# First layer's weight decode: words in PSUM, ranked first and in program order, eight staging areas

## The chip, the cores and the metric

One core of a Trainium2 chip runs the whole program in one launch. The metric is the device time in microseconds (us), the median over runs. Engines are named as in the profile: PE (matmul), PEld (its weight loads), DVE (VectorE), ACT (ScalarE), POOL (GpSimd), SP (SyncE, which here issues every DMA).

## The reference

Three stages follow one another, in fp32:

```python
for t in range(768):                       # 4 batches x 8 heads, head size 40
    y[:, :, t] = r_t @ state
    Sa = state @ a_t
    state = state * w_t - outer(Sa, b_t) + outer(v_t, k_t)
x = y.transpose(0, 2, 1, 3).reshape(3072, 320)
h = x @ w_in                               # first layer, 320 -> 2048, weights float64
x = (h * cos(h)) @ w_out                   # 2048 -> 320, float64
P = exp(x @ w_gate - max); 8 rounds of row and column normalisation
out = sum_e P[:, e] * (relu(x @ w1[e]) @ w2[e])    # second layer, 8 experts, 320 -> 1024 -> 320
```

## The kernel before

The recurrence is cut into 24 chunks of 32 steps. A chunk has three parts: `early(n)` (L664) loads its inputs, scans the decays, forms small matrices, writes them to DRAM and reads them back (tensor `LD`), and has POOL invert them with 62 instructions (`inverse`, L707; result through DRAM tensor `UD`); `late(n)` (L722) fetches that result and builds transposed operands; `chain(n)` (L764) runs the matmuls that carry the state from chunk to chunk, and ends with two stores to the DRAM tensor `XT` (recorded as group "y").

The first layer works in 12 passes of 256 tokens, `moe1(i)` (L940). Pass i needs the `XT` of chunks 2i and 2i+1, and all 16 weight slots `wt1`. Per pass PE does 128 matmuls 128x256 (`l1`) and 96 of 128x320 (`l2`); results go to the DRAM tensor `ZD`. Its work buffers lie in the tiles `fs` and `r2`.

The weights of the first layer arrive as float64 words. `moe1_weights` (L852) decodes 32 blocks, 16 of `w_in` (128x384) and 16 of `w_out` (128x320), in turn. A block is loaded by one DMA into a staging area; `decode` (L535) takes five DVE instructions and one ACT instruction, with an intermediate `t` that lies beside the words in the staging area; ACT rounds the upper part, PE subtracts it from the exact sum by three matmuls into a PSUM bank of pool "A" (`low`, L866), and ACT copies the rest. There are three staging areas, two in `fs` and one in `at2`; the last eight blocks use only the one in `at2` (`PREP_FS`, L575), because `fs` is the passes' by then.

The second layer (`moe2`, L1069) runs 8 experts x 6 groups of 512 tokens on the same engines, after the passes.

Nothing is issued in the order of the code. `Recorder` collects all operations with their dependences, and `order` (L353) plans each engine's order by list scheduling with costs of its own: at each step the engine that is free first takes, of its ready operations, the one with the smallest key. The key is made of the group's entry in `PRIORITY` (L578): first the rank, then, where the second entry is a number, the negative length of the longest path behind the operation (plus that many thousand ns), and where it is None, the operation's place in the program:

```python
r, base, slope = PRIORITY.get(o[6]) or PRIORITY[o[6][0]]
key.append((r, i, 0) if base is None else (r, -tail[i] - 1e3 * (base + slope * o[6][1]), i))
```

PSUM banks are given out in the same plan: pool "A" has four, for the attention, the decode and the second layer's first products; "M" and "N" have two each. Where the plan has PE idle before 800 us, it puts filler matmuls there (`fill`, 64x64 from the constants). The chip then runs each engine's list in that order, each instruction waiting for its semaphores; SP's list is in order too, so a DMA that waits holds back all DMAs behind it. All instructions are issued from one line (L519), so the profile tells them apart by tiles: `XT<-at` is a chunk's result, `ZD<-fs` a pass's, `fs<-in_win`, `at<-in_win`, `fs<-in_moe_w_out` and `at<-in_moe_w_out` are loads of float64 blocks.

Of the kernel before, what the change touches and what calls it, by code (L numbers as in the profile page):

```python
# [6 lines left out]
F32 = mybir.dt.float32  # L7
F32R = mybir.dt.float32r
# [113 lines left out]
class Lazy:  # L122


    def __init__(self, get, sample, region, chain=()):
        self.get, self.sample, self.reg, self.chain = get, sample, region, chain
# [408 lines left out]
def decode(nc, expo, st, t, rest=None, sign=1):  # L535

    lo, hi = st[:, :, 0], st[:, :, 1]
    e = t.bitcast(I32)
    nc.vector.tensor_scalar(e, hi, 20, 0x7FF, op0=ALU.logical_shift_right, op1=ALU.bitwise_and)
    nc.scalar.activation(e, e, AF.Relu, scale=float(2 ** 23), bias=expo)  # L540
    nc.vector.scalar_tensor_tensor(e, hi, -2 ** 31, e, op0=ALU.bitwise_and, op1=ALU.bitwise_or)
    nc.vector.tensor_scalar(hi, hi, 3, 0x7FFFFF, op0=ALU.logical_shift_left, op1=ALU.bitwise_and)
    nc.vector.tensor_tensor(hi, hi, e, op=ALU.bitwise_or)
    rest = t if rest is None else rest
    nc.vector.scalar_tensor_tensor(rest, lo.bitcast(mybir.dt.uint32), sign * 2.0 ** -52, t, op0=ALU.mult, op1=ALU.mult)
    return hi.bitcast(F32), rest


def sinkhorn(nc, ident, P, sk, red, ones, bank):
# [22 lines left out]
        nc.vector.tensor_tensor(P, P, red.unsqueeze(1).to_broadcast([128, 24, 8]), op=ALU.mult)  # L572


PREP_FS = 24  # L575


PRIORITY = {  # L578
    "chain": (0, 0, 0), "y": (1, 0, 0), "early": (1, 0, 0), "late": (1, 0, 0), "prep": (1, 275, 0),
    "one": (1, 0, 0), "gate": (2, 0, 0), "two": (3, None, 0), "fetch": (4, None, 0),  # L580
}
SLOT = 1280
NR1 = 10
# [5 lines left out]
R2_COLS = 1536 + 2048 + 40  # L589
# [3 lines left out]
class Kernel:  # L593
    def __init__(self, sb, ps, dr, a):
        self.a, self.dr = a, dr
        tile = lambda n, c, dt: sb.tile([128, c], dt, tag=n, name=n)
        r1a = tile("r1a", NR1 * SLOT, F32R)
        r1b = tile("r1b", ACC_COLS, F32R)
        self.r2 = tile("r2", R2_COLS, F32R).bitcast(F32)
        self.fs = tile("fs", FS_COLS, F32)  # L600
        self.cst = tile("cst", CONSTS.shape[1], F32)
        self.at1 = tile("at1", AT1_COLS, F32)
        self.at2 = tile("at2", AT2_COLS, F32)
        self.flag = tile("flag", NCH + 2, F32)
        self.nc = nc = Recorder(ps, {"A": (4, 5, 6, 7), "M": (0, 1), "N": (2, 3)}, {x.name for x in a.values()})
        slots = lambda t, n: [t[:, SLOT * i:SLOT * i + SLOT] for i in range(n)]
        ra, rb = slots(r1a.bitcast(F32), NR1), slots(r1b.bitcast(F32), 6)
        self.wt1 = ra + rb
        self.acc = nc.later(r1b, F32, lambda: tile("r1b", ACC_COLS, F32)).rearrange("p (t d) -> p t d", d=DM)
        z = nc.later(self.at1, F32R, lambda: tile("at1", AT1_COLS, F32R)).bitcast(F32)  # L610
        self.zT_all = z[:, 0:ZT_COLS].rearrange("p (t k c) -> p t k c", t=6, k=6)
        self.w2s = [z[:, ZT_COLS + SLOT * i:ZT_COLS + SLOT * i + SLOT] for i in range(NAT)] + ra
        nc.sync.dma_start(out=self.cst, in_=a["consts"])
        self.c = {k: self.cst[:, o:o + w] for k, (o, w) in CONST_COLS.items()}
        nc.fill(self.c["ident"])
        ui = self.c["uinit"]
        self.uinit = bass.AP(ui.tensor, ui.offset + 28, [ui.ap[0], [-4, 8], [1, C]])
        self.nident = tile("nident", 128, F32R)
        self.XT = dr.tile([DM, NT], F32, name="XT")
        self.ZD = dr.tile([NT, DM], F32, name="ZD")  # L620
# [231 lines left out]
    def moe1_weights(self):  # L852

        nc, a = self.nc, self.a
        sets = [self.fs[:, 0:1152], self.fs[:, 1152:2304], self.st]
        self.used = 0

        def stage():
            k = self.used % 3 if self.used < PREP_FS else 2
            self.used += 1  # L860
            return sets[k]

        nident = self.nident
        nc.scalar.activation(nident, self.c["ident"], AF.Copy, scale=-1.0)

        def low(A, hi, Bl):  # L866

            ps = nc.bank("A")[:, 0:A.shape[1]]
            nc.tensor.matmul(ps, lhsT=self.c["ident"], rhs=A, start=True, stop=False)
            nc.tensor.matmul(ps, lhsT=nident, rhs=hi, start=False, stop=False)  # L870
            nc.tensor.matmul(ps, lhsT=nident, rhs=Bl, start=False, stop=True)
            return ps

        for f in range(16):
            nc.group = ("prep", f)
            w = self.wt1[f]
            s = stage()
            st = s[:, 0:768].bitcast(I32).rearrange("p (c w) -> p c w", w=2)
            nc.sync.dma_start(
                out=s[:, 0:768].bitcast(I32), in_=a["win"].bitcast(I32)[f])  # L880
            A, Bl = decode(nc, self.c["expo"], st, s[:, 768:1152], w[:, 384:768].bitcast(F32R), -1)
            hi = w[:, 0:384].bitcast(F32R)
            nc.scalar.activation(hi, A, AF.Copy)
            ps = low(A, hi, Bl)
            nc.scalar.activation(w[:, 384:640].bitcast(F32R), ps[:, 0:256], AF.Copy)
            nc.scalar.activation(w[64:128, 256:384].bitcast(F32R), ps[64:128, 256:384], AF.Copy)
            s = stage()
            st = s[:, 0:640].bitcast(I32).rearrange("p (c w) -> p c w", w=2)
            nc.sync.dma_start(out=s[:, 0:640].bitcast(I32), in_=a["moe_w_out"].bitcast(I32)[128 * f:128 * f + 128, :])
            A, Bl = decode(nc, self.c["expo"], st, s[:, 640:960], w[:, 960:1280].bitcast(F32R), -1)  # L890
            hi, lo = w[:, 640:960].bitcast(F32R), w[:, 960:1280].bitcast(F32R)
            nc.scalar.activation(hi, A, AF.Copy)
            nc.scalar.activation(lo, low(A, hi, Bl), AF.Copy)
# [417 lines left out]
```

## Time and profile before

| | |
|---|---|
| median of 3 runs | 2336.92 us (2335.42 to 2342.84) |
| profiled execution | 2336.27 us |
| its span, first to last instruction | 2334.5 us |
| busy: PE, DVE, ACT, POOL | 98%, 45%, 35%, 29% |

Times in the trace are us from the span's start. A view by windows gives, for each stretch, the busy us and the number of instructions of every engine, then PE's granted clock (1.00 is full), the DMA engines' busy share and GB/s. A view by groups gives the engine, the operation, the tiles written and read, the shape and count, and then busy us, mean ns of one, and the idle time in front. SPq rows are DMA issues: start, us that the issue took, tiles. PE's busy time holds the filler, so it is not all work.

### The profile page before, as it was taken

The numbers are of one execution on the slowest core, as the hardware profiler recorded it, in microseconds if no ns is written. First come the engines' busy times: TensorE is split into PE (matmuls) and PEld (weight loads), VectorE is DVE, ScalarE is ACT, GpSimd is POOL, SyncE is SP. The second block draws the span as 40 slices with busy tenths as digits, with TensorE's granted clock in tenths as the row PEclk, the third lists the DMA queues.
The fourth block names the chain that finished last, engine by engine and source line by source line (L and its number), as shares of the span: only waits on it lengthen the run. The fifth ranks groups of instructions, "written<-read, shape, count | busy, mean of one in ns | idle before, by whom it ended". The sixth has DMA issues, their size and how long they took to land.

```text
span 2334.5 us, 45995 instructions
## 1 busy us (share of the span) xinstructions
PE 2278.6 (98%) x18893; PEld 2082.4 (89%) x18893; DVE 1057.3 (45%) x2106; ACT 820.9 (35%) x1710; POOL 685.8 (29%) x1694
## 2 busy tenths in 40 slices
PE   8999999999999999999999999999999999999997
PEld 8899898898998998899998888999999999999886
DVE  7667888778887654511222222222222222222222
ACT  4436565466655655324112112112112112112111
POOL 5867766588746613002002002002002002001000
PEclk9999998999998999999999999999999999999998
DMA  6434343434443215001001001001001001000000
GB/s 172 111 100 113 88 116 81 98 91 105 100 97 80 64 48 143 6 1 51 1 1 50 1 1 51 1 1 51 1 1 50 1 1 50 1 1 7 23 23 24
DMA packets 155497, 116.86 MB, mean 50 GB/s; under 512 B 112528, under 2 KB 134032, under 8 KB 153360
## 3 DMA queue, kind: packets, MB, share of 16 engines
q1 hardware_dynamic: 155280, 113.86, 19.4%
q8 instruction: 150, 2.46, 0.5%
q14 instruction: 67, 0.55, 0.1%
HBM read 95.73 MB, written 18.09 MB: 49 GB/s over the span
## 4 chain that ended last, share of the span: by engine, by line


## 5 line engine op out<-in xcount | busy, mean ns | idle before, releaser
L519 DVE SCALAR_TENSOR_TENSOR r<-ps,r 128x512 fp32r<-128x512 f32 x384 | 265.3, 691 | 972.2 <-ACT r L519 971.7
L519 PE MATMUL ps<-r1a,r 128*128 128x320 f32 x4248 | 672.4, 310 | 1.7 <-ACT fs L519 1.6
L519 PEld LDWEIGHTS ps<-r1a,r 128*128 128x128 f32 x4248 | 637.5, 188 | 17.4 <-ACT fs L519 2.3
L519 ACT ACTIVATE r<-ps 128x512 fp32r<-128x512 f32 x480 | 286.1, 596 | 1032.1 <-PE ps L519 1009.5
L519 POOL TENSOR_TENSOR at<-at 128x60 f32<-128x60 f32 (+24 forms) x1488 | 545.4, 367 | 261.3 <-DMA at<-LD 123.2
L519 PE MATMUL ps<-at,r1a 128*128 128x512 f32 x2352 | 578.7, 397 | 0.0
L519 PEld LDWEIGHTS ps<-at,r1a 128*128 128x128 f32 x2352 | 436.2, 188 | 94.1 <-issue 0.2
L519 PE MATMUL ps<-at 128*64 128x72 f32 (+6 forms) x6064 | 458.1, 252 | 17.5 <-DVE at L519 6.5
L519 PEld LDWEIGHTS ps<-at 80*64 80x64 f32 (+4 forms) x6064 | 394.1, 150 | 63.3 <-DVE at L519 9.6
L519 POOL TENSOR_TENSOR r1a<-at,r1a 128x256 fp32r<-128x256 f32 (+2 forms) x147 | 101.2, 691 | 832.9 <-ACT r1a L519 823.6
L519 PE MATMUL ps<-at,r 128*128 128x320 f32 (+1 forms) x1128 | 182.4, 313 | 0.0
L519 PEld LDWEIGHTS ps<-at,r 128*128 128x128 f32 (+1 forms) x1128 | 167.3, 184 | 9.7
L519 PE MATMUL ps<-cst 128*64 128x64 f32 x2520 | 167.2, 225 | 4.6 <-DMA cst<-in_consts 4.6
L519 PEld LDWEIGHTS ps<-cst 128*64 128x64 f32 x2520 | 156.5, 140 | 14.0 <-issue 7.4
L519 PE MATMUL ps<-r,r1a 128*128 128x256 f32 x960 | 139.2, 294 | 2.2 <-DVE r L519 2.2
L519 ACT ACTIVATE at<-ps 80x320 f32<-80x320 f32 (+4 forms) x234 | 92.4, 416 | 126.2 <-PE ps L519 123.5
L519 POOL TENSOR_TENSOR at<-at,at 128x256 fp32r<-128x256 f32 (+2 forms) x45 | 31.0, 692 | 348.3 <-ACT at L519 346.6
L519 PEld LDWEIGHTS ps<-r,r1a 128*128 128x128 f32 x960 | 126.2, 197 | 4.7 <-DVE r L519 3.3
L519 DVE TENSOR_TENSOR at<-ps,at 80x160 f32<-80x160 f32 (+4 forms) x396 | 100.7, 316 | 21.0 <-ACT at L519 20.6
L519 ACT ACTIVATE at<-at,cst 64x256 f32<-64x256 f32 (+3 forms) x160 | 88.7, 584 | 39.2 <-PE ps L519 20.5
L519 DVE SCALAR_TENSOR_TENSOR r1b<-ps,fs,r1b 128x320 f32<-128x320 f32 x168 | 80.9, 544 | 36.9 <-PE ps L519 36.9
L519 DVE SCALAR_TENSOR_TENSOR fs<-ps,fs 128x512 f32<-128x512 f32 x96 | 65.8, 685 | 53.1 <-ACT fs L519 52.5
(74 smaller groups left out, 1458.8 us busy)
## 6 DMA issues: line engine op xcount, KB each, us to landing
at<-in_w SPq DMA_DIRECT2D x64, 352.0 KB
at<-in_tabk SPq DMA_DIRECT2D x24, 640.0 KB
at<-LD SPq DMA_DIRECT2D x96, 128.0 KB
at<-in_trv SPq DMA_DIRECT2D x24, 480.0 KB
at<-in_tw SPq DMA_DIRECT2D x24, 165.3 KB
at<-in_nv SPq DMA_DIRECT2D x48, 80.0 KB
ZD<-fs SPq DMA_DIRECT2D x24, 160.0 KB
at<-ZD SPq DMA_DIRECT2D x24, 160.0 KB
```

What stands on the lines that cost most here:

```text
L519: getattr(getattr(nc, self.ENGINES[e]), method)(*[res(x) for x in args], **{n: res(x) for n, x in kwargs.items()})
```

## The change

The decode's intermediate `t` moves from the staging area to a bank of PSUM pool "A". Staging areas shrink to 768 columns and become eight: three in `fs`, four in the tile of `r2`, one in `at2`, used in turn for all 32 blocks; `r2` becomes the passes' buffer once its last staging use is over. In the plan the decode ("prep") gets rank 0 and program order instead of rank 1 with 275 us of advance; the passes ("one") go from rank 1 to rank 0, and keep the order by path length.

```diff
-PREP_FS = 24
 PRIORITY = {
-    "chain": (0, 0, 0), "y": (1, 0, 0), "early": (1, 0, 0), "late": (1, 0, 0), "prep": (1, 275, 0),
-    "one": (1, 0, 0), "gate": (2, 0, 0), "two": (3, None, 0), "fetch": (4, None, 0),
+    "chain": (0, 0, 0), "y": (1, 0, 0), "early": (1, 0, 0), "late": (1, 0, 0), "prep": (0, None, 0),
+    "one": (0, 0, 0), "gate": (2, 0, 0), "two": (3, None, 0), "fetch": (4, None, 0),
 }
@@ Kernel.__init__
-        self.r2 = tile("r2", R2_COLS, F32R).bitcast(F32)
+        self.raw = tile("r2", R2_COLS, F32)
...
+        self.r2 = nc.later(self.raw, F32R, lambda: tile("r2", R2_COLS, F32R)).bitcast(F32)
@@ moe1_weights
-        sets = [self.fs[:, 0:1152], self.fs[:, 1152:2304], self.st]
+        sets = [t[:, 768 * i:768 * i + 768] for t, n in ((self.fs, 3), (self.raw, 4), (self.st, 1)) for i in range(n)]
...
         def stage():
-            k = self.used % 3 if self.used < PREP_FS else 2
             self.used += 1
-            return sets[k]
+            return sets[self.used % len(sets)]
...
-            A, Bl = decode(nc, self.c["expo"], st, s[:, 768:1152], w[:, 384:768].bitcast(F32R), -1)
+            A, Bl = decode(nc, self.c["expo"], st, nc.bank("A", False)[:, 0:384], w[:, 384:768].bitcast(F32R), -1)
...
-            A, Bl = decode(nc, self.c["expo"], st, s[:, 640:960], w[:, 960:1280].bitcast(F32R), -1)
+            A, Bl = decode(nc, self.c["expo"], st, nc.bank("A", False)[:, 0:320], w[:, 960:1280].bitcast(F32R), -1)
```

## Rows read from the trace of the kernel before

**Rows 1.** Windows: length, then busy us (instructions) by engine, PEclk, DMA share, GB/s.
```profile
core 0: us, PE busy (x) PEld busy (x) DVE busy (x) ACT busy (x) POOL busy (x), PEclk, DMA share, GB/s
0.00:60.00 60.00, 53.84 (x881) 50.32 (x882) 45.04 (x86) 26.92 (x64) 32.18 (x74) 0.97 0.67 168
60.00:140.00 80.00, 79.92 (x1150) 71.46 (x1151) 54.49 (x135) 36.58 (x90) 63.21 (x162) 1.00 0.43 110
140.00:300.00 160.00, 152.35 (x2180) 140.65 (x2178) 121.38 (x265) 87.56 (x204) 112.14 (x273) 0.99 0.43 104
300.00:835.00 535.00, 512.29 (x6381) 488.68 (x6377) 421.47 (x912) 312.67 (x703) 345.78 (x992) 0.96 0.38 89
835.00:906.00 71.00, 70.21 (x517) 67.18 (x516) 38.21 (x63) 46.90 (x90) 23.08 (x35) 1.00 0.33 98
```
**Rows 2.** PE groups of 0 to 300 us: the filler, and the passes' first products.
```profile
L519 PE MATMUL ps<-cst 128*64 128x64 f32 x2108 | 138.3, 225 | 4.6 <-DMA cst<-in_consts 4.6
L519 PE MATMUL ps<-r,r1a 128*128 128x256 f32 x128 | 19.7, 296 | 1.5 <-DVE r L519 1.5
L519 PE MATMUL ps<-r,r1b 128*128 128x256 f32 x48 | 7.6, 292 | 0.0
```
**Rows 3.** The same groups of 300 to 835 us.
```profile
L519 PE MATMUL ps<-r,r1a 128*128 128x256 f32 x672 | 98.2, 296 | 0.2 <-DVE r L519 0.2
L519 PE MATMUL ps<-r,r1b 128*128 128x256 f32 x432 | 63.2, 294 | 0.4 <-DVE r L519 0.4
L519 PE MATMUL ps<-cst 128*64 128x64 f32 x412 | 28.8, 224 | 0.0
```
**Rows 4.** SP's issues in order of time: results of chunks 0, 1, 5, 23; the last pass's.
```profile
96.81 1.28 SPq L519 DMA_DIRECT2D XT<-at  x2
...
139.30 1.27 SPq L519 DMA_DIRECT2D XT<-at  x2
...
286.06 1.27 SPq L519 DMA_DIRECT2D XT<-at  x2
...
834.38 1.27 SPq L519 DMA_DIRECT2D XT<-at  x2
...
905.08 0.42 SPq L519 DMA_DIRECT2D ZD<-fs  x1
```
**Rows 5.** SP's issues: some loads of blocks, and chunk 0's LD and UD.
```profile
15.59 0.39 SPq L519 DMA_DIRECT2D LD<-at  x1
...
25.78 2.81 SPq L519 DMA_DIRECT2D at<-LD  x4
...
60.84 0.33 SPq L519 DMA_DIRECT2D fs<-in_moe_w_out  x1
...
71.78 0.33 SPq L519 DMA_DIRECT2D fs<-in_win  x1
...
73.08 2.62 SPq L519 DMA_DIRECT2D UD<-at  x4
...
142.19 0.35 SPq L519 DMA_DIRECT2D at<-in_moe_w_out  x1
...
266.33 0.36 SPq L519 DMA_DIRECT2D at<-in_moe_w_out  x1
```
**Rows 6.** SP's own waits, 30 to 140 us: total us, times, longest.
```profile
SPq L519 <- PE ps L519: 64.4, 21, 10.0
```
**Rows 7.** POOL in order of time: the first three inverses, run together.
```profile
30.90 87.91 POOL L519 TENSOR_TENSOR at<-at 128x31 f32<-128x31 f32 x186 [22.42 <-DMA at<-LD]
```
**Rows 8.** DVE groups by shape: decode steps; last, a subtraction reading PSUM.
```profile
L519 DVE TENSOR_SCALAR fs<-fs 128x384 int32<-128x384 int32 x16 | 6.1, 381 | 3.8 <-DMA fs<-in_win 3.6
L519 DVE TENSOR_TENSOR fs<-fs 128x384 int32<-128x384 int32 x8 | 5.0, 625 | 0.0
L519 DVE SCALAR_TENSOR_TENSOR fs<-fs 128x384 int32<-128x384 int32 x8 | 4.5, 559 | 6.7 <-ACT fs L519 6.7
L519 DVE TENSOR_TENSOR at<-ps,at 128x384 fp32r<-128x384 f32 x24 | 13.1, 554 | 20.8 <-ACT at L519 20.6
```
**Rows 9.** Windows (columns as in Rows 1), one early stretch.
```profile
20.00:25.00 5.00, 5.00 (x82) 5.00 (x80) 4.18 (x7) 0.09 (x1) 0.00 (x0) 0.66 0.97 263
```

## Prediction

> **What bounds the kernel now.** I read the windows first, then PE's groups by stretch, then SP's issues in time, then POOL and DVE. The windows [rows 1] show PE busy nearly throughout, which misleads: of its busy time before 300 us, 138.3 us is filler [rows 2], work that stands for idleness. From 300 to 835 us the filler is only 28.8 us [rows 3]. So there are two regimes. After 300 us the engines are full: chunks 5 to 23 end at 286.06 and 834.38 us [rows 4], 548.3 / 18 = 30.5 us per chunk, and in the 535 us the passes issue 672 + 432 = 1104 first products [rows 3], 1104 / 128 = 8.6 of 12 passes, or 0.49 pass per chunk. Before 300 us PE has room, but the passes issue only 128 + 48 = 176 products [rows 2], 1.4 passes. The remaining 12 - 8.6 - 1.4 = 2.0 passes run after the last chunk, from 834.38 to 905.08 us [rows 4], 35 us each. The second layer only starts in earnest behind them, and the change doesn't touch it.
>
> Why so little before 300 us? A pass needs all 32 blocks decoded. Nine of their loads are issued after 140 us, from 142.19 to 266.33 us, since the last eight blocks share one staging area [rows 5]; chunk 1, the other condition of pass 0, is there at 139.30 us [rows 4]. Pass 0 thus waits some 130 us for its last weights. SP shows a second price of few areas: four block loads, issued from 60.84 to 71.78 us, stand ahead of chunk 0's UD store, issued at 73.08 us [rows 5]; the first of the three inverses, 87.91 / 3 = 29.3 us each from 30.90 us [rows 7], was over at about 60.2 us. SP spends 64.4 of 110 us waiting for PE, mostly for areas that PE's subtraction frees [rows 6]. So 73.1 - 60.2 = 13 us of chunk 0 is a queue standing still.
>
> **The change part by part.** The work of the decode stays: 32 DMAs, 160 DVE, 112 ACT and 96 PE instructions; it moves.
>
> *Eight areas, decode first.* A 384-column block costs DVE 0.381 x 2 + 0.559 + 0.625 + about 0.6 = 2.5 us [rows 8], a 320-column one 320/384 of it, 2.1, so 2.3 on average. The nine blocks now later than 140 us are 9 x 2.3 = 21 us of DVE; DVE is idle 15.0 + 25.5 = 40.5 us before 140 us [rows 1]. They fit: I expect the last block near 120 us, and pass 0 to wait for chunk 1 alone. The cover is that idle time; without it the excess delays the chunks one for one (below).
>
> *The start.* Eight loads instead of three now stand on SP and in the transfers ahead of chunk 0's inputs: 4 x 384 + 4 x 320 = 2816 KB (128 partitions of 768 or 640 words) against 1088, 1728 KB more. At the 263 GB/s of a full stretch [rows 9] that is 6.6 us. And eight decodes, ranked before `early(0)`, can take DVE 8 x 2.3 = 18 us. So POOL's start moves from 30.90 by 6.6 to 25 us; I take 13, near the lower end, because a decode waits for ACT in its middle and `early` slips in there. The LD round trip, issued at 15.59 and 25.78 us [rows 5], already waits behind loads, so it is not shortened. POOL then starts at 44 us and ends its second inverse at 44 + 58.6 = 103 us. From the UD store to the result chunk 0 took 96.81 - 73.08 = 23.7 us [rows 4, 5]. With SP no longer held, chunk 1 could end at 103 + 24 = 127 us; with the whole lag of before (139.30 minus the second inverse's end at 89.5, 50 us) at 153. I take 135 us, in the lower half, since the block loads behind which SP stood are gone by then.
>
> *From there the full regime.* 22 chunks at 30.5 us end at 135 + 671 = 806 us; 22 x 0.49 = 10.8 passes go with them, the last 1.2 take 42 us: 848 us against 905, a gain of 57. Each us of chunk 1's end is one us of this.
>
> *t in PSUM.* Each decode now holds two of the four banks of pool A in turn, one from its first DVE instruction to its last, one from PE's subtraction to ACT's copy. What is queued behind is `early` and `chain`'s wish for a bank, during the first 120 us only. Its bounds: nothing, or what a decode's length of 2.3 us per chunk adds to chunks 0 to 2, 7 us. The DVE instructions with `t`: the nearest row that reads PSUM, 554 ns, stands between the 559 and 625 ns of the same size in SBUF [rows 8], so between -0.07 and 0 us each; three per block make at most 7 us less. I take 0 for both.
>
> The first instruction is the exception to weigh. It runs at 381 ns from SBUF to SBUF [rows 8]. The Trainium skill, "VectorE: DVE Perf Modes", section "Why PSUM operands drop a tier", says that any PSUM operand leaves an fp32 `tensor_scalar` at the single rate. No row here has such an instruction with PSUM; if the rule holds it goes to about 554 ns, 32 x 0.17 = 5.5 us of DVE in all, an estimate, and the decode would end by that much later, still before chunk 1.
>
> *"one" to rank 0.* The passes now go before `early`, `late` and "y" on every engine. That is new through the whole 700 us: what is queued behind a pass is the next chunks' preparation, and behind it POOL's inverse, 29.3 us per chunk [rows 7] against a cadence of 30.5. Nothing of before shows the price. Below it is bounded by nothing (DVE is idle 21% in the full regime [rows 1], enough to let preparation through), above by the whole of a pass's 35 us once per two chunks; I take 2 us per pair, near the lower end because chain, which has rank 0 by path length, is not pushed back. 11 pairs make 22 us.
>
> Sum: 57 - 22 = 35 us. The profiled execution took 2336.3 us, 1.8 more than its span and 0.6 less than the median; 2336.3 - 35 = 2301 us.
>
> **The rivals.** *The full gain* (against it: only the new order; for it: DVE and POOL both have idle time): chunk 1 at 130 us, nothing lost to the order, 62 us, 2274 us.
>
> *A late start.* Decode takes DVE whole for its 32 x 2.3 = 74 us and preparation of chunks 1 and 2 waits. For it: rank 0 before rank 1, and room in eight areas to keep DVE fed. Chunk 1 then ends at 153 us: 57 - 18 - 22 = 17 us, 2319 us.
>
> *No change.* DVE, not PE, is what is full: 421.47 of 535 us, 79%, against (45.04 + 54.49 + 121.38) / 300 = 74% before 300 us [rows 1]. If 79% is a ceiling, the first 300 us shrink only to 220.9 / 0.79 = 280: 20 us, and the 22 of the order take them back: 2338 us.
>
> *Slower.* Passes in rank 0 run in one piece, preparation starts only behind them, POOL's inverse of 29.3 us after that, and the chain meets an empty pipeline once per pair while PE has no backlog of passes to fill it, as it has now with 2.0 passes left at the end. It decides from 57 / 11 = 5.2 us per pair on; at 7.5 us the loss is 83 us, the net 26: 2362 us. For it: POOL has hardly 1 us of slack per chunk. Against it: a pass keeps DVE only about half busy after 835 us, 38.21 of 71 us [rows 1].
>
> **How the numbers follow.** Forecast 0.46; full gain 0.18; late start 0.10; no change 0.07; slower 0.19. About 0.3%, 7 us, is what a measurement of this kernel can tell from no change. Faster: 0.46 + 0.18 + 0.08 of the late start = 0.72; same: 0.07 + 0.02 = 0.09; slower 0.19. The forecast's own range is 2288 to 2318 (one to three us per pair, and the 7 us of the banks). The range for 8 in 10 takes in the full gain with 6 us to spare, and the slower case up to 6.5 us per pair (72 - 57 = 15 us): 2268 to 2352.
>
> **What would show it.** Right: the last load of a block before 120 us; POOL's first inverse at 38 to 56 us; UD of chunk 0 within a few us of the first inverse's end; chunk 1 by 127 to 153 us; over two passes' products and far less filler before 300 us; about one pass after the last chunk. Wrong: chunk 1 after 160 us; POOL gaps and filler that come back between passes after 300 us with a cadence over 33 us per chunk; or a second layer whose length changes, which nothing here foresees.

## The result, and the profile after

The change takes 2306.14 us (median of 4 runs, 2299.16 to 2313.61) against 2339.11 us for the kernel before in the same comparison: ratio 0.986, 95% interval 0.982 to 0.9899, 33 us. 2301 us and a gain of 35 us were forecast. The sum came out; its two largest terms were not worth by themselves what they were put at, as the experiments show.

The profiled execution has a span of 2300.5 us. Behind the last pass's store it takes 2300.5 - 869.5 = 1431 us, before 2334.5 - 905.1 = 1429 us: the second layer is as it was, and all of the difference lies ahead of it. The windows answer to [rows 1]:

```profile
core 0: us, PE busy (x) PEld busy (x) DVE busy (x) ACT busy (x) POOL busy (x), PEclk, DMA share, GB/s
0.00:60.00 60.00, 54.17 (x796) 47.62 (x797) 52.53 (x103) 34.31 (x82) 16.11 (x38) 1.00 0.90 228
60.00:140.00 80.00, 78.84 (x1157) 71.17 (x1155) 62.97 (x152) 36.13 (x86) 56.84 (x177) 1.00 0.41 100
140.00:300.00 160.00, 158.29 (x2040) 150.07 (x2039) 129.23 (x274) 100.85 (x225) 97.48 (x264) 1.00 0.41 96
300.00:835.00 535.00, 519.32 (x6726) 497.11 (x6726) 417.65 (x898) 310.70 (x704) 359.67 (x1031) 0.99 0.38 90
```

DVE works 115.5 us of the first 140 instead of 99.5, and PE's clock is 0.99 instead of 0.96 from 300 to 835 us. PE's groups of 0 to 300 us, the filler and the passes' first products, answer to [rows 2]:

```profile
L519 PE MATMUL ps<-cst 128*64 128x64 f32 x1548 | 103.3, 226 | 4.3 <-DMA cst<-in_consts 4.1 <-issue 0.2
L519 PE MATMUL ps<-r,r1a 128*128 128x256 f32 x240 | 34.6, 289 | 0.0
...
L519 PE MATMUL ps<-r,r1b 128*128 128x256 f32 x112 | 16.0, 287 | 0.0
```

352 products stand there instead of 176, and 560 fewer filler matmuls. From 300 to 835 us the same groups [rows 3] show no more passes than before, 659 + 418 = 1077 products against 1104, and twice the filler, so that most of what was filled before 300 us comes back behind it:

```profile
L519 PE MATMUL ps<-r,r1a 128*128 128x256 f32 x659 | 96.3, 292 | 3.1 <-ACT r L519 2.1 <-DVE r L519 0.8
...
L519 PE MATMUL ps<-r,r1b 128*128 128x256 f32 x418 | 62.4, 292 | 1.0 <-DVE r L519 0.9
L519 PE MATMUL ps<-cst 128*64 128x64 f32 x850 | 58.7, 224 | 0.0
```

SP's issues in order of time answer to [rows 4, 5]:

```profile
77.11 2.62 SPq L519 DMA_DIRECT2D UD<-at  x4
...
145.31 0.63 SPq L519 DMA_DIRECT2D XT<-at  x1
146.04 0.55 SPq L519 DMA_DIRECT2D fs<-in_moe_w_out  x1
...
176.61 2.92 SPq L519 DMA_DIRECT2D fs<-XT  x3
...
256.81 1.27 SPq L519 DMA_DIRECT2D XT<-at  x2
...
823.46 1.27 SPq L519 DMA_DIRECT2D XT<-at  x2
...
869.51 0.32 SPq L519 DMA_DIRECT2D ZD<-fs  x1
```

Chunk 1 comes 6 us later (145.31 us), chunk 5 29 us earlier (256.81), chunk 23 11 us earlier (823.46); from the last chunk's first store to the last pass it takes 46 us instead of 71. The last block is loaded at 146.04 us and pass 0 loads its tokens at 176.61 us. What stands in front of that load is the decode itself: PE's last subtraction of a block in `fs`, where the tokens go, starts at 175.2 us (the second of the two in this row):

```profile
174.91 0.73 PE L519 MATMUL ps<-fs,cst 128*128 128x320 f32 x2
```

POOL's first three inverses [rows 7]:

```profile
49.83 74.88 POOL L519 TENSOR_TENSOR at<-at 128x31 f32<-128x31 f32 x186 [41.34 <-DMA at<-LD]
```

### The profile page after: what moved, and what is told of

It is laid out like the page before. It is cut to its first block, busy times and chain, and to the rows that moved or that the text cites. A ratio compares the mean times of both kernels' runs of the same rounds, so it can differ in the third digit from the quotient of the medians.

```text
span 2300.5 us, 45714 instructions
## 1 busy us (share of the span) xinstructions
PE 2258.6 (98%) x18773; PEld 2064.7 (90%) x18773; DVE 1058.9 (46%) x2106; ACT 820.1 (36%) x1710; POOL 658.8 (29%) x1694
## 4 chain that ended last, share of the span: by engine, by line
## 5 line engine op out<-in xcount | busy, mean ns | idle before, releaser
L519 POOL TENSOR_TENSOR at<-at 128x60 f32<-128x60 f32 (+24 forms) x1488 | 518.1, 348 | 276.0 <-DMA at<-LD 160.2
L519 PE MATMUL ps<-at 128*64 128x72 f32 (+6 forms) x6064 | 446.4, 248 | 11.8 <-DMA at<-UD 4.6
L519 PEld LDWEIGHTS ps<-at 80*64 80x64 f32 (+4 forms) x6064 | 385.1, 147 | 54.7 <-issue 8.2
L519 PE MATMUL ps<-cst 128*64 128x64 f32 x2400 | 162.3, 225 | 4.3 <-DMA cst<-in_consts 4.1
L519 PEld LDWEIGHTS ps<-cst 128*64 128x64 f32 x2400 | 149.9, 139 | 14.0 <-issue 5.8
L519 DVE TENSOR_TENSOR at<-ps,at 80x256 f32<-80x256 f32 (+4 forms) x396 | 103.3, 317 | 19.3 <-ACT at L519 18.7
L519 ACT ACTIVATE fs<-ps,cst 128x512 int32<-128x512 f32 x96 | 65.7, 684 | 88.0 <-PE ps L519 78.6
```

The lines of the kernel that those rows point to most:

```text
L519: getattr(getattr(nc, self.ENGINES[e]), method)(*[res(x) for x in args], **{n: res(x) for n, x in kwargs.items()})
```

## The experiments

Twelve kernels ran beside the kernel before. The table has, for each, the median, the ratio to before, the median clock of its runs, and, from its profiled execution, the passes' first products before 300 us (in passes, of 128), chunk 23's second store, the last pass's store and the time between them. Each ratio is taken against runs of before made beside it. The profiled execution can lie up to 8 us off its kernel's median: that of e2 is 7 us above it, those of e1 and e5 are 6 below, so the last three columns compare two kernels to some 10 us.

| kernel | us | ratio, 95% | clock | passes by 300 | chunk 23 | last pass | between |
|---|---|---|---|---|---|---|---|
| before | 2335.5 (54 runs) | | 0.986 | 1.4 | 835 | 905 | 70 |
| the change | 2306.1 | 0.986 [0.982, 0.9899] | 0.9935 | 2.8 | 824 | 870 | 46 |
| e1 areas | 2334.8 | 0.9992 [0.9968, 1.0017] | 0.9855 | 1.0 | 807 | 895 | 88 |
| e2 areas, decode first | 2332.8 | 0.9969 [0.994, 0.9997] | 0.9805 | 1.5 | 821 | 910 | 89 |
| e3 areas, passes first | 2317.2 | 0.9903 [0.9869, 0.9937] | 0.993 | 1.5 | 840 | 887 | 47 |
| e4 both ranks, 3 areas | 2322.6 | 0.9937 [0.9917, 0.9957] | 0.9945 | 1.1 | 847 | 893 | 46 |
| e5 passes first, 3 areas | 2341.7 | 1.0027 [1.0013, 1.004] | 0.9885 | 1.0 | 858 | 905 | 47 |
| e6 before, replanned | 2338.6 | 1.0019 [0.9992, 1.0045] | 0.9855 | 1.5 | 841 | 912 | 71 |
| e7 the change, replanned | 2317.2 | 0.9914 [0.9885, 0.9943] | 0.992 | 2.7 | 843 | 895 | 52 |
| e8 chunk 0 ahead | 2291.5 | 0.9814 [0.9791, 0.9837] | 0.9925 | 2.4 | 816 | 864 | 48 |
| e9 four areas | 2313.6 | 0.9907 [0.988, 0.9934] | 0.9925 | 1.9 | 842 | 891 | 49 |
| e10 no filler after 300 | 2315.4 | 0.9916 [0.9888, 0.9944] | 0.977 | 2.6 | 843 | 891 | 48 |
| e11 e8, replanned | 2299.8 | 0.985 [0.9826, 0.9875] | 0.9945 | 2.4 | 823 | 871 | 48 |
| e12 more chunks ahead | 2301.4 | 0.9865 [0.9838, 0.9893] | 0.994 | 1.4 | 821 | 869 | 48 |

**e1: the areas and PSUM alone.** From the changed kernel:

```diff
-"prep": (0, None, 0), "one": (0, 0, 0)
+"prep": (1, 275, 0), "one": (1, 0, 0)
```

> Eight areas and the words in PSUM, but the ranks of before. Theory A (the passes start earlier because the last blocks are decoded earlier, and areas are what the decode lacked): last block loaded before 170 us, pass 0 done by 260 us, 10 to 30 us faster than before. Theory B (the ranks do it, the areas do nothing by themselves): within 7 us of before. Theory C (any new plan differs by this much, through PE's clock and where the stalls fall): anywhere from 35 us faster to 10 slower, with no relation to when pass 0 ends.

Nothing is gained: 0.9992. The areas and the words in PSUM do bring the work forward: the last block is loaded at 213 us instead of 266, chunk 5 ends at 264 us instead of 286 and chunk 23 at 807 instead of 835. But pass 0 ends at 321 us, later than before, and 88 us of work are left behind the last chunk. Theory A fails in this form.

**e2: the decode first, the passes as before.** From the changed kernel:

```diff
-"one": (0, 0, 0)
+"one": (1, 0, 0)
```

> The change with the passes left in rank 1. Theory A: the same as the change within 10 us, since the decode's order and areas are kept; if my price for the passes' rank (22 us) was real, up to 22 us faster than the change, about 2285 us. Theory B: within 7 us of before if it is the passes' rank that does it. Theory C: anything between 2300 and 2340 us.

Hardly anything is gained, 0.9969, though the last block is loaded at 146 us and pass 0 fetches its tokens at 178 us, both as in the change. SP's issues of e2: pass 0's load and last store, the last chunk, the last pass:

```profile
178.36 1.62 SPq L519 DMA_DIRECT2D fs<-XT  x3
...
292.43 0.35 SPq L519 DMA_DIRECT2D ZD<-fs  x1
...
820.17 1.27 SPq L519 DMA_DIRECT2D XT<-at  x2
...
909.77 0.32 SPq L519 DMA_DIRECT2D ZD<-fs  x1
```

Pass 0 ends at 292 us, in the change at 247. PE's groups from 178 to 248 us, first of e2, then of the change (the filler and the first products in each):

```profile
L519 PE MATMUL ps<-cst 128*64 128x64 f32 x178 | 14.3, 247 | 0.0
L519 PE MATMUL ps<-r,r1a 128*128 128x256 f32 x80 | 11.0, 289 | 0.0
...
L519 PE MATMUL ps<-r,r1b 128*128 128x256 f32 x48 | 6.9, 290 | 0.4 <-DVE r L519 0.4
```

```profile
L519 PE MATMUL ps<-r,r1a 128*128 128x256 f32 x128 | 18.9, 291 | 0.0
...
L519 PE MATMUL ps<-r,r1b 128*128 128x256 f32 x48 | 6.6, 287 | 0.0
...
L519 PE MATMUL ps<-cst 128*64 128x64 f32 x65 | 4.4, 223 | 0.0
```

The weights are there in both. With the passes in rank 1, PE does 128 products and 178 fillers; in rank 0, 176 products and 65 fillers. So decoding early is of little use while the passes stand behind `early` and `late`. This run decides against the largest term of my sum as priced by itself.

**e3: the passes first, the decode as before.** From the changed kernel:

```diff
-"prep": (0, None, 0)
+"prep": (1, 275, 0)
```

> The change with the decode left in rank 1 with its 275 us of advance. Theory A: decode is done somewhat later than in the change, chunk 0 a little earlier, 10 to 35 us faster than before. Theory B with the passes' rank as the cause: the whole gain, 33 us. Theory B with the decode's rank as the cause: within 7 us of before.

The ratio is 0.9903, 18 us less than e1: within theory A's range and about half of theory B's 33 us. Against e1, with which it shares all but the passes' rank, chunk 23 comes 33 us later and the work behind it is 41 us shorter.

**e4: the ranks alone.** From the kernel before, three areas:

```diff
-"prep": (1, 275, 0), "one": (1, 0, 0)
+"prep": (0, None, 0), "one": (0, 0, 0)
```

> The kernel before with the two new ranks, three areas and the words in SBUF. Theory A: the last eight blocks still go through one area, so the last load is after 200 us, pass 0 ends after 260 us, within 10 us of before; SP stands behind block loads, so chunk 0 or 1 may be later than before. Theory B: 25 to 35 us faster. Theory C: anything.

The ratio is 0.9937, 13 us by the medians: less than theory B, more than A allows. The last load is at 294 us and pass 0 ends at 316 us, as A said. So the two ranks gain something without any early block. What sets e4 apart from e5 below, which has the passes' rank alone and loses, is the decode's own rank: PE's last subtraction starts at 306 us here and at 333 us in e5, where the decode stands behind the passes. The decode's rank alone was not run.

**e5: the passes' rank alone.** From the kernel before:

```diff
-"one": (1, 0, 0)
+"one": (0, 0, 0)
```

> The kernel before with one edit: the passes in rank 0. After the first four runs: with the passes in rank 1 (before, e1, e2) PE's clock averaged 0.976 to 0.988, with them in rank 0 (the change, e3, e4) 0.993 to 0.995. Theory D (the passes' rank keeps PE from standing idle on the way to a pass's next product, so its clock falls less often, and this is about half of the gain): clock 0.992 or more, 10 to 20 us faster than before. Theory A (early decode alone): within 7 us of before. Theory C (any new plan differs so): no rule.

The kernel is slower, 1.0027, at a clock of 0.9885: theory D fails for the gain. SP's issues of e5, the last chunk and the last pass:

```profile
857.08 1.27 SPq L519 DMA_DIRECT2D XT<-at  x2
...
905.28 0.32 SPq L519 DMA_DIRECT2D ZD<-fs  x1
```

The rank exchanges 23 us behind the last chunk against 23 us of later chunks, and the last pass ends at 905.28 us, where it ended before [rows 4]. With early blocks the exchange is another: from e2 to the change chunk 23 comes 3 us later and 43 us go behind it, though some 11 us of these 40 are only that the profiled execution of e2 lies above its kernel's median and that of the change below.

**e6 and e7: the same kernels planned anew.** In before and in the change:

```diff
-SLACK = 200
+SLACK = 210
```

> The kernel before with a neutral change to the plan: the slack that the planner allows PE after other engines is 210 instead of 200 ns. Theory D: clock 0.976 to 0.989 again, within 10 us of before. Theory C: a clock of 0.992 or more, or over 15 us either way, turns up here as well.

> The changed kernel with the same neutral change to the plan. Theory D: clock 0.992 or more, within 10 us of the change (2296 to 2316 us). Theory C: it can fall back to 2335 us and a clock of 0.986.

Before keeps its time (2338.6 us), the change loses 11 us (2317.2 us, 1 us outside what theory D allowed). A plan's details are thus worth up to some 10 us, and differences of that size between two plans, e4 against e9 for instance, prove nothing. All three kernels that were planned with the 210 became slower (3, 11 and 8 us, the third is e11), so that the constant need not be neutral. None moved by the 35 us that theory C allowed to any plan. The 27 us from e2 to the change are above it, and 16 remain to the replanned version; e1 to e5 were not replanned.

**e8 and e11: chunk 0 ahead of the decode.** In the changed kernel (e11 with the slack of 210 as well):

```diff
-"gate": (2, 0, 0),
+"gate": (2, 0, 0), ("early", 0): (0, 0, 0), ("late", 0): (0, 0, 0), ("early", 1): (0, 0, 0),
```

> The changed kernel with early(0), late(0) and early(1) put into rank 0 ahead of the decode. If the start (POOL at 49.8 instead of 30.9 us) costs what chunk 1's 145 instead of 139 us say, the chunks come 5 to 15 us earlier and the end by as much, 2291 to 2301 us. If pass 0 waits for the last blocks rather than for chunk 1, no gain: within 7 us of the change.

> e8 with the neutral change to the plan (slack 210). The same edit took the change from 2306 to 2317 us and before from 2335.5 to 2338.6. If e8's 2291 us is the start and not one lucky plan: 2290 to 2305 us, at least 8 us faster than e7 (2317).

2291.5 us and, replanned, 2299.8: 15 and 17 us less than the change under the same plan settings. This version beats both kernels. The edit puts the first preparation ahead on every engine, not only in SP's list. In the profiled executions chunk 1 ends 6 us earlier than in the change, pass 0 ends 2 us later, and the last pass ends 5 us earlier; the rest of the 10 us between these two executions lies behind it. So how much of the gain is the start itself stays open. POOL starts 13 us earlier than in the change:

```profile
36.50 77.48 POOL L519 TENSOR_TENSOR at<-at 128x31 f32<-128x31 f32 x186 [28.02 <-DMA at<-LD]
```

**e9: four areas.** In the changed kernel:

```diff
-for t, n in ((self.fs, 3), (self.raw, 4), (self.st, 1)) for i in range(n)]
+for t, n in ((self.fs, 3), (self.st, 1)) for i in range(n)]
```

> The change with four staging areas of 768 columns instead of eight (three in fs, one in at2; the tile of r2 is left alone). So far areas alone gave nothing (e1) and the ranks with three areas and one for the last eight blocks gave 13 us (e4). Theory E (passes in rank 0 use what is decoded early; both are needed, and what counts is that the last blocks are there when chunk 1 is): four areas used to the end already bring the last load to about 170 us, and 2305 to 2320 us. If the eight areas as such count: 2320 us or more.

2313.6 us, last load at 170 us, as theory E said; it lies between the change and its own replanned version, so four areas can't be told from eight. PE's last subtraction starts at 202 us, and pass 0's tokens are loaded at 202.08.

**e10: no filler after 300 us.** In the changed kernel:

```diff
-FILL_END = 8e5
+FILL_END = 3e5
```

> The changed kernel with PE's filler left out after 300 us of the plan (850 filler matmuls in the trace of the change). It costs no useful work, so it measures the clock's part alone. If the clock is worth what runs of one kernel show among themselves (1.9 us per 0.001 of mean clock, over 46 runs of before), and without filler it falls from 0.9935 to 0.98, then 26 us slower than the change, 2332 us. If the filler does nothing for the clock: within 5 us of the change.

The clock fell to 0.977, further than expected, and the time rose by 9 us (13 by the ratios), not by 26; that is neither of the two cases. Windows of 300 to 843 us, of e10 and then of the change:

```profile
300.00:843.00 543.00, 497.14 (x5917) 475.47 (x5911) 419.85 (x905) 306.80 (x698) 350.00 (x1034) 0.92 0.37 86
```

```profile
300.00:843.00 543.00, 527.32 (x6787) 504.85 (x6787) 422.54 (x906) 317.82 (x719) 364.40 (x1039) 0.99 0.39 91
```

**e12: chunks 0 to 3 ahead.** In the changed kernel:

```diff
-"gate": (2, 0, 0),
+"gate": (2, 0, 0), **{(g, n): (0, 0, 0) for g, m in (("early", 4), ("late", 3)) for n in range(m)},
```

> As e8, but early of chunks 0 to 3 and late of chunks 0 to 2 all in rank 0 ahead of the decode. If chunk 1 still holds pass 0: chunk 1 before 138 us and 2283 to 2292 us. If the decode now ends later than chunk 1 and holds pass 0: pass 0 loaded after 180 us, 2291 to 2310 us.

2301.4 us, the second case: last load at 179 us, PE's last subtraction and pass 0's load at 228. Only 1.4 passes run before 300 us, as many as before the change, and still the kernel is some 32 us faster than before by its ratio: its chunk 6 ends at 288 us, against 317 before and 309 in the change. So passes run early are not the only use that can be made of the first 300 us; chunks run early serve as well. And e4, with 1.1 passes by 300 us and its chunk 6 where it was before (318 us), gains 13 us with neither.

## Why the prediction was right in its sum and wrong in its terms

*What bounds the kernel* held in part. The gain lies ahead of the second layer, and before 300 us 2.75 passes run instead of 1.4. But filler that came back after 300 us was named as a sign of being wrong, and it did come back (28.8 to 58.7 us), though the cadence rose only from 30.5 to 31.5 us per chunk and not over 33. From the start to the last pass PE's time divides so, first before, then in the change:

```profile
0.00:905.50 905.50, 868.11 (x11092) 817.89 (x11093) 680.53 (x1457) 510.20 (x1149) 576.38 (x1535) 0.97 0.41 99
L519 PE MATMUL ps<-cst 128*64 128x64 f32 x2520 | 167.2, 225 | 4.6 <-DMA cst<-in_consts 4.6
```

```profile
0.00:869.80 869.80, 845.42 (x10963) 798.82 (x10963) 680.73 (x1454) 508.43 (x1149) 550.04 (x1537) 0.99 0.43 103
L519 PE MATMUL ps<-cst 128*64 128x64 f32 x2400 | 162.3, 225 | 4.3 <-DMA cst<-in_consts 4.1 <-issue 0.2
```

The same split for other runs, up to each one's last pass (other matmuls are PE's busy time without the filler; idle is the rest; there are nearly as many of them in every run, 8550 to 8579):

| kernel | last pass, us | filler | other matmuls | idle | PE's clock |
|---|---|---|---|---|---|
| before | 905.5 | 167 | 701 | 37 | 0.97 |
| the change | 869.8 | 162 | 683 | 24 | 0.99 |
| e1 | 895.3 | 170 | 688 | 37 | 0.98 |
| e2 | 910.1 | 142 | 726 | 42 | 0.95 |
| e3 | 887.2 | 176 | 684 | 27 | 0.99 |
| e4 | 893.4 | 185 | 686 | 22 | 0.99 |
| e5 | 905.6 | 181 | 693 | 31 | 0.98 |
| e10 | 891.6 | 104 | 723 | 64 | 0.94 |

So of the 36 us by which the last pass ends sooner, only 5 are filler; 13 are time in which PE stood idle, and 18 are the other matmuls, which took less time each. Time found before 300 us was therefore not the gain by itself.

*The sum, term by term.* In the trace of the change it looks borne out: 149 products, 1.16 passes, are left behind chunk 23, 1.2 were forecast; the last pass ends at 870 us, which is the forecast 848 and the 22 of the order. This is in part luck: the decode was 55 us later than put, chunk 1 10 us, and the runs with one edit each show that neither term has its price by itself.

*The start.* POOL's start was put at 44 us (38 to 56): 49.83. SP's standing still at chunk 0 was said to go: the first inverse ends at 49.83 + 74.88 / 3 = 74.8 us, an estimate, and UD is issued at 77.11, 2 us later instead of 13. For the second and third inverse, which the prediction did not name, the same lag falls from 27 and 37 us to some 7. Chunk 1 does not profit, later chunks do: chunk 5 ends at 257 to 264 us in the change, e1, e2 and e3, with eight areas, whatever the ranks, and at 279 to 293 in before, e4 and e5, with three. Chunk 1, put at 135 us (127 to 153), came at 145.31. That the start has a price agrees with e8, which is 15 us faster.

*The decode* was expected to be through near 120 us, and pass 0 to wait for chunk 1 alone. That step failed: PE's last subtraction is at 175.2 us, and pass 0's tokens are loaded at 176.61 us, 31 us after chunk 1's result. The load follows the last subtraction in `fs` by 4 us or less in 12 of the 14 profiled kernels (all but e1 and e3). The sum had asked only for room on DVE, and DVE was done with that block at 155.9 us and ACT at 157.5. PE ran filler in between, so that the plan held the subtraction back; for what, a bank of PSUM for instance, is not shown.

*"From there the full regime"*, 57 us, is the main step that failed. It took for granted that the passes would run as soon as their weights and tokens were there. e1 and e2 have the areas, e2 the early decode as well, and they gain 2 and 7 us by their ratios, because the passes stay behind the chunks' preparation. In the table above e2 has less filler than the change up to the last pass; what it has more is 17 us of idle PE and 43 us of longer matmuls.

*"one" to rank 0* was a loss of 22 us in the sum. Alone it does cost, 6 us (e5). On top of early blocks it is what gains: 0.9903 against 0.9992 from e1 to e3, 0.986 against 0.9969 from e2 to the change, 18 and 27 us between the medians. The early decode and the passes' rank are worth little or less than nothing one by one and 20 to 33 us together (the replanned version and the change, by their ratios), and my sum had added them as if each stood by itself; that it came to 35 us is then no merit of its terms. Early blocks are not the only condition: e4 has the two ranks without them and gains 13 us. The rival "slower", in which passes in rank 0 push the chunks back, is what e5 does to the chunks: chunk 23 by 23 us, as much as the sum had put. It is paid for behind the last chunk, where the rank takes 23 to 43 us away: that time is 46 to 52 us in every run with the passes in rank 0, and 70 to 89 in every run without.

*t in PSUM* was taken at nothing. The row that reads PSUM, 554 ns, lies just below the 559 and 625 ns between which the prediction put it. The rows of the changed kernel on DVE, 128x384:

```profile
L519 DVE TENSOR_SCALAR ps<-r 128x384 int32<-128x384 int32 x8 | 4.5, 558 | 1.9 <-ACT r1b L519 1.7
L519 DVE SCALAR_TENSOR_TENSOR ps<-r,ps 128x384 int32<-128x384 int32 x8 | 4.4, 550 | 1.0 <-ACT ps L519 1.0
L519 DVE TENSOR_TENSOR r<-r,ps 128x384 int32<-128x384 int32 x8 | 4.4, 544 | 0.0
L519 DVE TENSOR_SCALAR r<-r 128x384 int32<-128x384 int32 x8 | 2.9, 367 | 0.1
```

The first instruction goes from 381 to 558 ns [rows 8], while the other `tensor_scalar` of a block, which stays in SBUF (last row), takes 367. This is as the Trainium skill, "VectorE: DVE Perf Modes", section "Why PSUM operands drop a tier", had it (554 was the estimate; the skill says it of fp32, and these are int32 words of the same size). The other two fall, from 559 and 625 ns to 550 and 544. What was missed is POOL. Its first three inverses take 87.9 to 89.5 us in the four profiled kernels with the words in SBUF (before, e4, e5, e6) and 73.6 to 77.5 in the ten with them in PSUM, whatever the ranks. One of each, e5 and e1:

```profile
32.31 88.14 POOL L519 TENSOR_TENSOR at<-at 128x31 f32<-128x31 f32 x186 [23.83 <-DMA at<-LD]
```

```profile
39.33 75.38 POOL L519 TENSOR_TENSOR at<-at 128x31 f32<-128x31 f32 x186 [30.84 <-DMA at<-LD]
```

That is 13 us by which POOL makes up its late start: 19 us behind at the first inverse, 6 at the end of the third (124.7 against 118.8 us). The Trainium skill, "SBUF — State Buffer", section "Who interferes with whom", says that VectorE and GpSimd share a pair of SBUF ports, which a VectorE instruction with two SBUF inputs takes and one with a single SBUF input, outside the two-port modes, does not. The times agree with it: three of a decode's five DVE instructions had two SBUF inputs and now have one. No run here has PSUM words with three areas, so the areas' share in it was not separated, and that the ports are the reason is argued, not shown.

*The clock* was not in the sum. It is 0.9935 instead of 0.986. Runs of before among themselves differ by 1.9 us per 0.001 of clock (54 runs, correlation -0.92), which would make 14 of the 33 us. When e10, without filler, takes the clock down by 0.0165, it costs 9 us, 0.6 per 0.001, which would make 4 us. But the second figure is a balance: in e10 the other matmuls take 40 us more and PE is idle 40 us more, and 58 us of filler are gone. The 18 us of other matmuls decide for the first figure, in the two profiled executions (clock 0.986 and 0.995): their time multiplied by PE's clock is the same, 674 to 680 us, in all rows of the table but e2 (690), an estimate that makes most of the 18 us clock, half of the gain in these two executions. Why the clock fell less, the filler after 300 us or the shorter idle times, was not separated. And the clock goes with the passes' rank: with filler it is 0.9885 to 0.9945 in all nine kernels that have them in rank 0, and 0.9805 to 0.986 in all four that do not. In e5 this alone gains nothing, since the time goes into filler (181 us instead of 167).

## What to carry to other kernels

Work that is made ready earlier was worth little here until whoever uses it was let ahead; where a change does both, the two terms can't be added, and each has to be priced with the other in place. A plan's price must be weighed against replanning: one small constant moved this kernel by 11 us. Filler that goes away in one stretch may come back in the next, so that it has to be counted up to the end of the stage. And where loads and decodes go ahead of everything, the first chunk's own preparation has to stand in front of them: that gave another 15 us.

## What the runs showed of the hardware

In one place the clock falls right after PE stands idle, in the middle of a full stretch. Windows of the kernel before, and PE in order of time:

```profile
392.00:398.00 6.00, 5.54 (x76) 5.10 (x75) 5.92 (x16) 2.36 (x6) 1.93 (x3) 1.00 0.02 4
398.00:404.00 6.00, 3.58 (x34) 3.43 (x33) 5.70 (x18) 4.99 (x13) 0.00 (x0) 0.66 0.37 76
404.00:410.00 6.00, 5.97 (x64) 5.46 (x61) 5.97 (x10) 2.94 (x8) 0.00 (x0) 0.50 0.26 76
410.00:416.00 6.00, 6.00 (x59) 5.38 (x60) 4.05 (x8) 1.33 (x4) 0.00 (x0) 0.50 0.43 104
```

```profile
397.60 1.37 PE L519 MATMUL ps<-at 128*80 128x72 f32 x16 [0.46 <-ACT at L519]
401.39 2.34 PE L519 MATMUL ps<-at 80*80 80x32 f32 x16 [2.42 <-DVE at L519]
```

PE waits 2.42 us for DVE, and from 404 to 416 us the granted clock is 0.50, the lower of its two levels (1.2 of 2.4 GHz); in the first six of these us DVE is busy 5.97. A wait and a low clock thus come together in this place; which of the two comes from the other elsewhere, it does not show.
